# Means and power moved one step up, second weights loaded three pieces ahead, in a fused attention and feed-forward kernel

## The chip, the cores and the metric

The kernel runs on one core of a Trainium2 chip. The metric is the device time of one execution in microseconds; a lower time is better. TensorE (PE) does the matrix products, VectorE (DVE), ScalarE (ACT) and GpSimd (POOL) the elementwise work, and SyncE (SP) issues the transfers between HBM and SBUF.

## What is computed

Attention over normalised queries and keys, for 8 batches of 12 heads with 448 rows of 64, and then a feed-forward over the 3584 rows of 768 that it yields:

```python
def rmsnorm(x, g):
    rms = np.sqrt(np.mean(x * x, axis=-1, keepdims=True) + 1e-06)
    return x / rms * g
q_n, k_n = (rmsnorm(q, g_q), rmsnorm(k, g_k))
scores = scale * np.matmul(q_n, k_n.transpose(0, 1, 3, 2))
attn = np.exp(scores - np.max(scores, axis=-1, keepdims=True))
attn = attn / (np.sum(attn, axis=-1, keepdims=True) + 1e-09)
x = np.matmul(attn, v)            # then (B,H,S,D) -> (B*S, H*D)
h = np.maximum(x @ w_in, 0.0)
out = h * h @ w_out
```

The weights `w_in` (768 x 2048) and `w_out` (2048 x 768) lie in HBM as 64-bit floats; the kernel turns them into 32-bit floats itself.

## The kernel before

**Pairs and steps.** The work is a list of 48 pairs: one batch and two heads each, six pairs to a batch. Each pair `i` takes four steps (`n` = 0 to 3), and in a step TensorE makes the scores of one quarter of the keys (`weigh`, L199), ScalarE their exponentials (L201), and TensorE the products with the values of the pair before (`attend`, L252) with the sums of the exponentials (L259 in the first batch, L263 later, there of sums that POOL and VectorE have added up, L215). The reciprocal of the sums is VectorE's (L274), and `finish` multiplies by it (xT, L283). TensorE's scores use banks 0 and 1 in even steps and 2 and 3 in odd ones.

**Queries and keys.** Before its scores a pair's queries and keys are squared by ScalarE (`square`, L138), summed to means by VectorE (`normalize`, L146 and L147), raised to the power -1/2 by POOL (rr, L151), and POOL multiplies the queries by it (qn, L156; the keys' factor goes into the exponential's scale). `turn` then transposes queries and keys on TensorE (L177) into banks 2 and 3; VectorE copies the turned queries out (qT, L179), ScalarE the keys (kT, L183). In the kernel before, pair i's steps hold for later pairs: the means, power and qn of pair i+1 in step 0, its transposes in step 2, and the squares of pair i+2 in step 3. The inputs of pair i+2 are issued in step 0 of pair i, behind the values of pair i.

**The weights** come in 56 pieces: 0 to 23 are the first weights (128 x 512), 24 to 55 the second (128 x 384). A piece is loaded as 64-bit words (`load_weights`, L386), split (`split_words`: ScalarE L402, POOL L403, ScalarE L407, and then POOL L409 for the first weights or ScalarE L414 for the second) and joined to 32 bits by three VectorE operations (`join_words`, L422, L426, L430). `convert(k)` joins piece k-1, loads a later piece and splits piece k; it runs once a step up to pair 6 and three times a step from pair 7 on. The first weights' words lie in the eight buffers tagged "h2", which the feed-forward uses for its activations later; the second weights' words lie in two buffers tagged "y", which it uses for its results. A load into a buffer waits until the piece that lay there is joined.

**The feed-forward** of a batch is cut into pieces (half a block of 128 hidden columns, six matrix instructions of L307; then L336 in groups of four blocks) that are put between the attention steps of the next batch, from the second pair on: about 2.8 pieces a step for the first batch. Its relu is ScalarE's (L316), the squares of it POOL's (L321, L326). It uses two banks by turns, so that a matmul waits for the relu two blocks earlier. The first pair of a batch has no feed-forward beside it.

Every engine runs its instructions in the order in which the program gives them, and so does SP's queue. The program's order is written out by hand.

Of the kernel before, what the change touches and what calls it, by code (L numbers as in the profile page):

```python
# [20 lines left out]
NJ = 4  # L21
# [52 lines left out]
def program(ctx, tc, q, k, v, g_row, moe_w_in, moe_w_out, out, shift):  # L74
# [5 lines left out]
    DM, DFF = moe_w_in.shape  # L80
    NC = DM // P
    NF = DFF // P
# [50 lines left out]
    def square(i):  # L133
        squares = [
            att.tile([CP, 2 * NJ, D], F32, name="squares", tag="squares") for _ in range(2)
        ]
        for x in range(2):
            nc.scalar.activation(squares[x], loaded[i][:, x], AF.Square)  # L138
        squared[i] = squares

    def normalize(i):

        qk = loaded.pop(i)
        ms = small.tile([CP, 4 * NJ], F32, name="ms", tag="ms", bufs=2)
        for x, squares in enumerate(squared.pop(i)):
            nc.vector.tensor_reduce(out=ms[:, ts(x, 2 * NJ)], in_=squares, axis=AX.X, op=ALU.add)  # L146
        nc.vector.tensor_scalar(  # L147
            out=ms, in0=ms, scalar1=1.0 / D, scalar2=1e-6, op0=ALU.mult, op1=ALU.add
        )
        rr = small.tile([CP, 2, 2 * NJ], F32, name="rr", tag="rr", bufs=4)  # L150
        nc.gpsimd.tensor_tensor(  # L151
            out=rr.rearrange("p x r -> p (x r)"), in0=ms,
            in1=minus_half.to_broadcast([CP, 4 * NJ]), op=ALU.pow,
        )
        qn = att.tile([CP, NJ, 2, D], F32, name="qn", tag="qn", bufs=1)
        nc.gpsimd.tensor_tensor(  # L156
            out=qn.rearrange("p j h d -> p h j d"),
            in0=qk[:, 0].rearrange("p (h j) d -> p h j d", j=NJ),
            in1=rr[:, 0].rearrange("p (h j) -> p h j", j=NJ)[:, :, :, None].to_broadcast([CP, 2, NJ, D]),
            op=ALU.mult,  # L160
        )
        kn = qk[:, 1]
        if shift:
            nc.gpsimd.tensor_tensor(
                out=kn, in0=kn, in1=rr[:, 1, :, None].to_broadcast([CP, 2 * NJ, D]), op=ALU.mult
            )
        normal[i] = qn, kn.rearrange("p (j h) d -> p j h d", h=2), rr[:, 1]

    def turn(i):

        qn, kn, _ = normal[i]
        qT = att.tile([P, S], F32, name="qT", tag="qT")
        kT = att.tile([P, S], F32, name="kT", tag="kT")
        for x, (dst, rows) in enumerate(((qT, qn), (kT, kn))):
            tr = banks[2 + x][:, 0:S]
            for j in range(NJ):
                nc.tensor.transpose(tr[:, ts(j, CP)], rows[:, j].rearrange("p h d -> p (h d)"), ident[:CP, :CP])  # L177
            if x == 0:
                nc.vector.tensor_scalar(  # L179
                    out=dst, in0=tr, scalar1=g, scalar2=None, op0=ALU.mult  # L180
                )
            else:
                nc.scalar.copy(dst, tr)  # L183
        turned[i] = qT, kT
# [92 lines left out]
    def finish(i):  # L277

        b, c = pairs[i]
        if c == 0:  # L280
            xts[b] = [None] * NC
        xT = ffn_p.tile([P, S], F32, name="xT", tag="xT", bufs=NC + 2)
        nc.vector.tensor_tensor(  # L283
            out=xT, in0=banks[4 + i % 2][:, 0:S], in1=dens.pop(i), op=ALU.mult
        )
        xts[b][c] = xT
        del turned[i], normal[i], values[i]
# [74 lines left out]
    def weight_chunks():  # L362

        n = DFF // 4
        for blk in range(4):
            for c in range(NC):
                yield w_in_sb[:, c, ts(blk, n)], moe_w_in[ts(c, P), :], blk * n
        for half in range(2):
            for f in range(NF):
                yield w_out_sb[:, f, ts(half, HALF)], moe_w_out[ts(f, P), :], half * HALF  # L370

    chunks = list(weight_chunks())
    words = {}

    def load_weights(k):
        if k >= len(chunks):
            return
        dst, rows, col = chunks[k]
        n = dst.shape[1]
        if rows.dtype == F32:  # L380
            nc.sync.dma_start(dst, rows[:, col : col + n])
            return

        tag, bufs = ("h2", NF // 2) if n == DFF // 4 else ("y", 2)
        words[k] = ffn_p.tile([P, n, 2], U32, name="words", tag=tag, bufs=bufs)
        nc.sync.dma_start(  # L386
            words[k].rearrange("p n w -> p (n w)"), rows.bitcast(U32)[:, 2 * col : 2 * (col + n)]
        )
# [9 lines left out]
    def split_words(k):  # L398
        if k not in words:
            return  # L400
        low, high = words[k][:, :, 0], words[k][:, :, 1]
        nc.scalar.activation(high.bitcast(F32), high.bitcast(F32), AF.Copy, scale=REBIAS)  # L402
        nc.gpsimd.tensor_scalar(  # L403
            out=high.bitcast(F32), in0=high.bitcast(F32), scalar1=MOST, scalar2=-MOST,
            op0=ALU.min, op1=ALU.max,
        )
        nc.scalar.activation(low.bitcast(F32), low, AF.Copy, scale=2.0**-29, bias=2.0**23)  # L407
        if k < 4 * NC:
            nc.gpsimd.tensor_scalar(  # L409
                out=low, in0=low.bitcast(F32), scalar1=-(2.0**23), scalar2=1.0,  # L410
                op0=ALU.add, op1=ALU.mult,
            )
        else:
            nc.scalar.activation(low, low.bitcast(F32), AF.Copy, bias=-(2.0**23))  # L414

    def join_words(k):
        if k not in words:
            return
        both = words.pop(k)
        low, high = both[:, :, 0], both[:, :, 1]  # L420
        bits = chunks[k][0].bitcast(U32)
        nc.vector.tensor_scalar(  # L422
            out=bits, in0=high, scalar1=4, scalar2=1,
            op0=ALU.logical_shift_left, op1=ALU.logical_shift_right,
        )
        nc.vector.scalar_tensor_tensor(  # L426
            out=bits, in0=high, scalar=0x80000000, in1=bits,
            op0=ALU.bitwise_and, op1=ALU.bitwise_or,
        )
        nc.vector.tensor_tensor(out=bits, in0=bits, in1=low, op=ALU.add)  # L430

    def convert(k):

        join_words(k - 1)
        if k + 3 < 4 * NC:
            load_weights(k + 3)
        elif k + 1 >= 4 * NC:
            load_weights(k + 1)
        split_words(k)

    load_qk(0)
# [16 lines left out]
    last = len(pairs) - 1  # L458

    with tc.manual_schedule(engines=ENGINES):  # L460
        square(0)
        normalize(0)
        turn(0)
        square(1)
        stream, pieces, done, piece = iter(()), 0, 0, 0
        for i, (b, c) in enumerate(pairs):
            for n in range(NJ):
                step = c * NJ + n
                if n == 0:
                    if i > 1 and not shift:  # L470
                        finish(i - 2)
                    load_v(i)
                    if i + 2 <= last:
                        load_qk(i + 2)
                if step == NJ and b:
                    stream, pieces, done = ffn(b - 1), ffn_pieces(b - 1), 0
                    while shift and piece <= len(chunks):
                        convert(piece)
                        piece += 1
                while shift and step == NJ and done < pieces or done * (steps - NJ) < pieces * (step - NJ + 1):  # L480
                    next(stream, None)
                    done += 1
                if shift and n == 0 and i:
                    for m in range(NJ):
                        attend(i - 1, m)
                    finish(i - 1)
                weigh(i, n)
                if i and not shift:
                    attend(i - 1, n)
                if i < last:  # L490
                    if n == 0:
                        normalize(i + 1)
                    if n == 2:
                        turn(i + 1)
                    if n == NJ - 1 and i + 2 <= last:
                        square(i + 2)
                for _ in range(1 if i < NPAIR + 1 else 3):
                    if piece <= len(chunks):
                        convert(piece)
                        piece += 1  # L500
            if c == NPAIR - 1:
                for _ in stream:
                    pass
        if not shift:
            finish(last - 1)
        for n in range(NJ):
            attend(last, n)
        finish(last)
        for _ in ffn(B - 1):
            pass  # L510
# [30 lines left out]
```

## Time and profile before

| what | value |
|---|---|
| median of 3 runs | 1763.82 us (1763.35 to 1767.3) |
| the profiled execution's own time | 1766.63 us |
| its span | 1764.8 us |
| TensorE (PE) busy | 1670.1 us, 95% of the span |
| VectorE (DVE) busy | 503.3 us, 29% |
| ScalarE (ACT) busy | 453.9 us, 26% |
| GpSimd (POOL) busy | 553.6 us, 31% |
| transfers | 70.24 MB, mean 40 GB/s |
| mean granted TensorE clock | 0.969 of full speed |

The shares are means over the whole run. In the profile's 40 slices TensorE is busy for 5 to 8 tenths in the first six slices (some 265 us), where the weights are converted, and for 9 tenths or more from there to the last one; the granted clock is below full speed in the same slices. "Idle before" in a row is the time an engine stood still before that instruction, and the arrow names what ended it.

### The profile page before, as it was taken

What the parts mean: (1) busy time and instruction counts of PE and PEld (TensorE: products, weight loads), DVE (VectorE), ACT (ScalarE), POOL (GpSimd) and SP (SyncE); (2) the same over time, 40 slices, a digit from 0 to 9 for tenths busy, and PEclk for the clock granted to TensorE, in tenths of its full rate; (3) what the DMA queues carried; (4) which work ended last, traced back from release to release, by engine and by line L of the source; (5) the groups of instructions that cost most, each with busy time, mean ns of one, the idle gap of its engine ahead of it and who ended that gap; (6) DMA issues with size and microseconds to landing.
All of it is one profiled execution on the core that took longest, in us unless ns stands there. A gap on an engine that the chain in (4) does not pass through costs nothing.

```text
span 1764.8 us, 14547 instructions
## 1 busy us (share of the span) xinstructions
PE 1670.1 (95%) x5516; PEld 781.7 (44%) x5516; DVE 503.3 (29%) x616; ACT 453.9 (26%) x829; POOL 553.6 (31%) x564
## 2 busy tenths in 40 slices
PE   5778789999999999999999999999999999999998
PEld 2223234534455344444455444544445444454554
DVE  4665453232222322232122322223222322221000
ACT  5553552132211322122211222122211222211100
POOL 5554443133311433224311333224421234212200
PEclk8878989999999999999999999999999999999999
DMA  5423431010010101110001100010011100000000
GB/s 183 155 97 80 112 105 43 25 41 16 17 34 25 40 16 32 34 41 16 16 25 34 40 16 16 25 49 16 20 30 32 34 22 26 14 15 9 0 19 20
DMA packets 80211, 70.24 MB, mean 40 GB/s; under 512 B 47876, under 2 KB 69380, under 8 KB 80132
## 3 DMA queue, kind: packets, MB, share of 16 engines
q1 hardware_dynamic: 80128, 69.23, 13.7%
q8 instruction: 45, 0.74, 0.2%
q14 instruction: 34, 0.28, 0.1%
q10 hardware_dynamic: 4, 0.00, 0.0%
HBM read 58.20 MB, written 11.01 MB: 39 GB/s over the span
## 4 chain that ended last, share of the span: by engine, by line
PE 83%; issue 5%; DVE 4%; POOL 3%; ACT 2%; DMA 2%; POOLq 0%; ACTq 0%; DVEq 0%; SPq 0%
PE bank L336 33%; PE bank L307 30%; PE bank L199 9%; PE bank L252 8%; DMA words<-in_moe_w_out_dram 2%; POOL rr L151 2%; PE bank L263 2%; PE bank L177 2%; DVE sum L215 1%; POOL words L403 1%; ACT wT L201 1%; DVE w_out_sb L426 1%; DVE qT L179 1%; ACT words L402 0%; DVE w_out_sb L422 0%
## 5 line engine op out<-in xcount | busy, mean ns | idle before, releaser
L307 PE MATMUL bank<-xT,w_in_sb 128*128 128x448 f32 x1536 | 611.8, 554 | 22.8 <-ACT h L316 20.9
L336 PE MATMUL bank<-w_out_sb,h 128*128 128x384 f32 x1792 | 593.9, 489 | 0.0
L336 PEld LDWEIGHTS bank<-w_out_sb,h 128*128 128x128 f32 x1792 | 335.4, 190 | 254.0 <-issue 32.2
L307 PEld LDWEIGHTS bank<-xT,w_in_sb 128*128 128x128 f32 x1536 | 291.2, 194 | 335.5 <-issue 287.7
L201 ACT ACTIVATE wT<-bank,rr 112x448 f32<-112x448 f32 x384 | 222.6, 631 | 536.9 <-PE bank L199 536.9
L199 PE MATMUL bank<-qT,kT 64*112 64x448 f32 x768 | 206.1, 616 | 25.9 <-DVE qT L179 25.3
L215 DVE TENSOR_TENSOR sum<-sum,wT 112x448 f32<-112x448 f32 x84 | 98.5, 1173 | 412.9 <-ACT wT L201 412.9
L215 POOL TENSOR_TENSOR sum<-sum,wT 112x448 f32<-112x448 f32 x84 | 98.8, 1176 | 359.6 <-ACT wT L201 358.5
L252 PE MATMUL bank<-wT,vt 112*64 112x448 f32 x768 | 194.6, 588 | 0.0
L316 ACT ACTIVATE h<-bank 128x448 f32<-128x448 f32 x128 | 69.0, 542 | 418.8 <-PE bank L307 418.8
L151 POOL TENSOR_TENSOR rr<-ms,minus_half 112x16 f32<-112x16 f32 x48 | 140.5, 2927 | 100.0 <-DVE ms L147 87.4
L215 DVE TENSOR_TENSOR sum<-wT 112x448 f32<-112x448 f32 x42 | 26.5, 632 | 483.1 <-PE bank L263 468.1
L274 DVE RECIPROCAL rden<-bank 128x448 f32<-128x448 f32 x48 | 141.6, 2951 | 13.7 <-PE bank L259 12.5
L215 POOL TENSOR_TENSOR sum<-wT 112x448 f32<-112x448 f32 x42 | 64.0, 1524 | 202.1 <-PE bank L263 202.1
L326 POOL TENSOR_TENSOR h<-h 128x448 f32<-128x448 f32 x64 | 59.7, 933 | 206.9 <-ACT h L316 206.9
L199 PEld LDWEIGHTS bank<-qT,kT 64*112 64x112 f32 x768 | 56.3, 181 | 143.8 <-issue 95.8
L321 POOL TENSOR_TENSOR h<-h 128x384 f32<-128x384 f32 x64 | 53.7, 839 | 164.3 <-ACT h L316 164.3
L252 PEld LDWEIGHTS bank<-wT,vt 112*64 112x64 f32 x768 | 39.5, 138 | 135.0 <-issue 131.3
L343 DVE COPY y<-bank 128x384 f32<-128x384 f32 x28 | 15.4, 549 | 257.8 <-PE bank L336 257.8
L345 ACT COPY y<-bank 128x384 f32<-128x384 f32 x28 | 13.4, 479 | 216.8 <-PE bank L336 204.2
L177 PE MATMUL bank<-ident,qn 112*128 112x112 f32 x192 | 30.9, 287 | 34.6 <-POOL qn L156 34.6
L403 POOL TENSOR_SCALAR words<-words 128x384 f32<-128x384 f32 (+1 forms) x56 | 37.0, 662 | 81.6 <-ACT words L402 80.1
(41 smaller groups left out, 672.6 us busy)
## 6 DMA issues: line engine op xcount, KB each, us to landing
words<-in_moe_w_in_dram SPq DMA_DIRECT2D x24, 512.0 KB, 5.0
words<-in_moe_w_out_dram SPq DMA_DIRECT2D x32, 384.0 KB, 3.2
qk<-in_q_dram SPq DMA_DIRECT2D x48, 224.0 KB, 3.0
qk<-in_k_dram SPq DMA_DIRECT2D x96, 112.0 KB, 3.3
vt<-in_v_dram SPq DMA_DIRECT2D x48, 224.0 KB, 2.8
out_dram<-y SPq DMA_DIRECT2D x8, 336.0 KB, 2.7
out_dram<-y SPq DMA_DIRECT2D x8, 288.0 KB, 2.6
out_dram<-y SPq DMA_DIRECT2D x8, 240.0 KB, 2.8
```

The lines of the kernel that those rows point to most:

```text
L151: nc.gpsimd.tensor_tensor(out=rr.rearrange("p x r -> p (x r)"), in0=ms, in1=minus_half.to_broadcast([CP, 4 * NJ]), op=ALU.pow,)
L177: nc.tensor.transpose(tr[:, ts(j, CP)], rows[:, j].rearrange("p h d -> p (h d)"), ident[:CP, :CP])
L199: nc.tensor.matmul(sc, lhsT=kT[r, ts(m, CP)], rhs=qT[r, :], start=True, stop=True)
L201: nc.scalar.activation(weights[i, e, m], sc, AF.Exp, scale=normal[i][2][:, 2 * m + e : 2 * m + e + 1])
L215: engine.tensor_tensor(out=sums[i, e], in0=so_far, in1=weights[i, e, m], op=ALU.add)
L252: nc.tensor.matmul(av[ds(e * D, D), :], lhsT=vt[:, e, m, :], rhs=weights[i, e, m], start=m == 0, stop=m == NJ - 1,)
L274: nc.vector.reciprocal(out=rden, in_=den)
L307: nc.tensor.matmul(ps, lhsT=w_in_sb[:, c, ts(f, P)], rhs=xT[c], start=c == 0, stop=c == NC - 1,)
L316: nc.scalar.activation(h[:, at : at + S], ps, AF.Relu)
L326: nc.gpsimd.tensor_tensor(out=full, in0=full, in1=full, op=ALU.mult)
L336: nc.tensor.matmul(ps, lhsT=h2[f][:, ts(n, P)], rhs=w_out_sb[:, f, ts(half, HALF)], start=f == 0, stop=f == NF - 1,)
L403: nc.gpsimd.tensor_scalar(out=high.bitcast(F32), in0=high.bitcast(F32), scalar1=MOST, scalar2=-MOST, op0=ALU.min, op1=ALU.max,)
```

## The change

`normalize` (means, power, qn) of pair i+2 now stands in step 3 of pair i, ahead of that step's scores and of the reciprocal of pair i-1; it stood in step 0 of pair i+1. `square` of pair i+2 stands in step 2, behind the transposes of pair i+1, and no longer behind step 3. `normalize(1)` is made ahead of the loop. `convert(k)` loads piece k+3 for all pieces; for the second weights it was piece k+1. The odd pieces of the second weights up to 47 get one of the eight "h2" buffers; the even ones and 49 to 55 stay in the two "y" buffers.

```diff
-        tag, bufs = ("h2", NF // 2) if n == DFF // 4 else ("y", 2)
+        early = n == DFF // 4 or k % 2 and k < len(chunks) - NF // 2
+        tag, bufs = ("h2", NF // 2) if early else ("y", 2)
         words[k] = ffn_p.tile([P, n, 2], U32, name="words", tag=tag, bufs=bufs)
...
         join_words(k - 1)
-        if k + 3 < 4 * NC:
-            load_weights(k + 3)
-        elif k + 1 >= 4 * NC:
-            load_weights(k + 1)
+        load_weights(k + 3)
         split_words(k)
...
         normalize(0)
         turn(0)
         square(1)
+        normalize(1)
...
+                if n == NJ - 1 and i + 2 <= last:
+                    normalize(i + 2)
                 if shift and n == 0 and i:
...
                 weigh(i, n)
                 if i and not shift:
                     attend(i - 1, n)
-                if i < last:
-                    if n == 0:
-                        normalize(i + 1)
-                    if n == 2:
-                        turn(i + 1)
-                    if n == NJ - 1 and i + 2 <= last:
+                if n == 2 and i < last:
+                    turn(i + 1)
+                    if i + 2 <= last:
                         square(i + 2)
```

On VectorE, one pair of the first stage, from the copy of the turned queries (qT_535) on. Before, with the reciprocal, a join, xT and only then the means (the rows L422, L426 and L430 are one join):

```order
L179 TENSOR_SCALAR qT_535<-bank2_107,g_101 128x448
L422 TENSOR_SCALAR w_in_sb_103<-words_440 128x512
L426 SCALAR_TENSOR_TENSOR w_in_sb_103<-words_440,w_in_sb_103 128x512
L430 ISA w_in_sb_103<-words_440,w_in_sb_103 128x1024
L274 RECIPROCAL rden_566<-bank6_111 128x448
L422 TENSOR_SCALAR w_in_sb_103<-words_465 128x512
L426 SCALAR_TENSOR_TENSOR w_in_sb_103<-words_465,w_in_sb_103 128x512
L430 ISA w_in_sb_103<-words_465,w_in_sb_103 128x1024
L283 TENSOR_TENSOR xT_581<-bank4_109,rden_566 128x448
L146 TENSOR_REDUCE ms_599<-squares_568 112x8
L146 TENSOR_REDUCE ms_599<-squares_569 112x8
L147 TENSOR_SCALAR ms_599<-ms_599 112x16
```

The same place in the changed kernel, whose lines L423, L427 and L431 are the join:

```order
L179 TENSOR_SCALAR qT_535<-bank2_107,g_101 128x448
L423 TENSOR_SCALAR w_in_sb_103<-words_444 128x512
L427 SCALAR_TENSOR_TENSOR w_in_sb_103<-words_444,w_in_sb_103 128x512
L431 ISA w_in_sb_103<-words_444,w_in_sb_103 128x1024
L146 TENSOR_REDUCE ms_560<-squares_547 112x8
L146 TENSOR_REDUCE ms_560<-squares_548 112x8
L147 TENSOR_SCALAR ms_560<-ms_560 112x16
L274 RECIPROCAL rden_578<-bank6_111 128x448
L423 TENSOR_SCALAR w_in_sb_103<-words_473 128x512
L427 SCALAR_TENSOR_TENSOR w_in_sb_103<-words_473,w_in_sb_103 128x512
L431 ISA w_in_sb_103<-words_473,w_in_sb_103 128x1024
L283 TENSOR_TENSOR xT_589<-bank4_109,rden_578 128x448
```

The two sums and the scaling of the means went from behind xT to ahead of the reciprocal; they are those of the pair after next.

On SP's queue, where the first weights' loads end and the second's begin (vt are the values, qk queries and keys). Before:

```order
L386 DMA words<-in_moe_w_in_dram 128x1024
L386 DMA words<-in_moe_w_out_dram 128x768
L127 DMA vt<-in_v_dram 112x2x256
L113 DMA qk<-in_q_dram 112x2x256
L118 DMA qk<-in_k_dram 112x4x64 x2
L386 DMA words<-in_moe_w_out_dram 128x768 x4
```

And in the changed kernel:

```order
L387 DMA words<-in_moe_w_in_dram 128x1024
L387 DMA words<-in_moe_w_out_dram 128x768 x3
L127 DMA vt<-in_v_dram 112x2x256
L113 DMA qk<-in_q_dram 112x2x256
L118 DMA qk<-in_k_dram 112x4x64 x2
L387 DMA words<-in_moe_w_out_dram 128x768 x4
```

Two more pieces of the second weights stand ahead of pair 6's values and the queries and keys of pair 8, and so it stays, two pieces more ahead, up to pair 9.

## Rows read from the trace of the kernel before

**Rows 1.** TensorE's waits over the span: total us, times, longest us.

```profile
PE bank L177 <- POOL qn L156: 34.6, 14, 9.0
PE bank L199 <- DVE qT L179: 25.3, 13, 3.5
PE bank L307 <- ACT h L316: 20.9, 7, 5.1
```

**Rows 2.** Stretches: length, busy us (count) by engine, granted clock, DMA share, GB/s.

```profile
40.15:118.97 78.82, 56.90 (x224) 18.99 (x224) 53.72 (x73) 42.77 (x76) 42.61 (x41) 0.78 0.39 127
154.33:273.49 119.16, 98.24 (x277) 42.14 (x277) 58.87 (x99) 61.91 (x124) 53.68 (x67) 0.90 0.38 104
599.30:686.55 87.25, 87.25 (x277) 38.14 (x276) 20.72 (x20) 22.35 (x40) 35.76 (x41) 1.00 0.06 16
```

**Rows 3.** Timeline of one first-stage pair: start, us, engine, line, operation, idle before.

```profile
84.14 2.96 DVE L274 RECIPROCAL rden<-bank 128x448 f32<-128x448 f32 x1 [2.54 <-PE bank L259]
...
86.61 1.01 PE L199 MATMUL bank<-qT,kT 64*112 64x448 f32 x4
...
87.02 0.36 DVE L422 TENSOR_SCALAR w_in_sb<-words 128x512 uint32<-128x512 uint32 x1
...
88.85 0.62 DVE L283 TENSOR_TENSOR xT<-bank,rden 128x448 f32<-128x448 f32 x1
...
89.20 1.01 PE L199 MATMUL bank<-qT,kT 64*112 64x448 f32 x4
...
89.39 1.27 DVE L146 TENSOR_REDUCE ms<-squares 112x8 f32<-112x512 f32 x2
...
90.95 3.01 POOL L151 TENSOR_TENSOR rr<-ms,minus_half 112x16 f32<-112x16 f32 x1 [5.63 <-DVE ms L147]
...
91.23 0.69 DVE L426 SCALAR_TENSOR_TENSOR w_in_sb<-words,w_in_sb 128x512 uint32<-128x512 uint32 x1
...
95.14 1.01 PE L177 MATMUL bank<-ident,qn 112*128 112x112 f32 x4 [3.27 <-POOL qn L156]
...
95.85 0.43 DVE L422 TENSOR_SCALAR w_in_sb<-words 128x512 uint32<-128x512 uint32 x1 [3.10 <-POOL words L403]
...
98.29 0.67 DVE L179 TENSOR_SCALAR qT<-bank,g 128x448 f32<-128x448 f32 x1
...
99.01 1.83 PE L199 MATMUL bank<-qT,kT 64*112 64x448 f32 x4 [2.12 <-DVE qT L179]
...
103.96 1.14 PE L199 MATMUL bank<-qT,kT 64*112 64x448 f32 x4
```

**Rows 4.** Timeline of TensorE: the last scores of pairs 1 and 6.

```profile
40.15 1.84 PE L199 MATMUL bank<-qT,kT 64*112 64x448 f32 x4 [2.92 <-DVE qT L179]
...
140.30 1.84 PE L199 MATMUL bank<-qT,kT 64*112 64x448 f32 x4 [3.51 <-DVE qT L179]
```

**Rows 5.** Timeline of the second stage: a late piece and the matmul behind it.

```profile
189.14 0.54 ACT L402 ACTIVATE words<-words 128x384 f32<-128x384 f32 x1 [4.57 <-DMA words<-in_moe_w_out_dram]
...
192.95 1.83 PE L307 MATMUL bank<-xT,w_in_sb 128*128 128x448 f32 x2 [5.11 <-ACT h L316]
```

**Rows 6.** DMA issues: count, KB each, median us from issue to landing.

```profile
words<-in_moe_w_in_dram SPq DMA_DIRECT2D x24, 512.0 KB, 5.0
words<-in_moe_w_out_dram SPq DMA_DIRECT2D x32, 384.0 KB, 3.2
...
qk<-in_k_dram SPq DMA_DIRECT2D x96, 112.0 KB, 3.3
```

**Rows 7.** Timeline: the first pair of batch 3 (from 0), and the scores of batch 4's.

```profile
584.23 2.95 DVE L274 RECIPROCAL rden<-bank 128x448 f32<-128x448 f32 x1
...
586.73 0.60 PE L177 MATMUL bank<-ident,qn 112*128 112x112 f32 x4 [1.34 <-POOL qn L156]
...
588.89 1.81 PE L199 MATMUL bank<-qT,kT 64*112 64x448 f32 x4 [1.18 <-DVE qT L179]
...
784.53 1.01 PE L199 MATMUL bank<-qT,kT 64*112 64x448 f32 x4 [1.18 <-DVE qT L179]
```

## Prediction

> **What bounds the kernel now.** I read the waits of TensorE first, then the stages, then one pair's timeline. TensorE waits for three things [rows 1]: the transposes for the normalised queries (POOL qn), the scores for the turned queries (DVE qT), and the feed-forward's matmuls for a relu on ScalarE. The stages tell where [rows 2]. In the first one (pairs 2 to 5, no feed-forward beside them) TensorE is busy 56.90 of 78.82 us at a mean granted clock of 0.78; in the second (first feed-forward, while the second weights are converted) 98.24 of 119.16 us at 0.90. The third row is the same amount of work as the second, two batches later: 28 feed-forward pieces and ten attention steps in 87.25 us, TensorE never idle. So the second stage loses 119.16 - 87.25 = 31.9 us, and the last half of the run has nearly nothing to give.
>
> One pair of the first stage [rows 3] shows the loop. The reciprocal of the sums starts at 84.14; behind it on VectorE stand a join of words, xT and the means (89.39); only then can POOL take the power (90.95, 3.01 us), then qn; the transposes start at 95.14 after 3.27 us of idle TensorE. That is not all: POOL's next half of a word split stood behind the power, so VectorE's join at 95.85 waited 3.10 for it, and qT (98.29) stands behind that join. The next scores start at 99.01, after another 2.12 idle, and run at the lower of the two clock levels (1.2 against 2.4 GHz): the step from there lasts 4.95 us (to 103.96), where a step with TensorE fed lasts 2.59 (86.61 to 89.20). A pair takes 78.82 / 4 = 19.7 us, of which TensorE needs four times 2.59 and about 1.2 for the transposes, 11.6.
>
> In the second stage the loads are late [rows 5]: ScalarE waits 4.57 us for a piece of the second weights, the relus behind it in its queue wait too, and the matmul that needs the relu's bank starts at 192.95 after 5.11 idle, at the lower clock.
>
> **Part 1: means and power one step up.** No instruction is added or taken away; square goes ahead of the third step's split, and means, power and qn go to step 3, a whole pair before their transposes. The wait for qn (3.27) then has three steps of cover, 7.8 us and more, against 4.2 from the power's start to the transposes, so I cost it at nothing. The wait of the join at 95.85 goes with it, because the split of that step no longer stands behind a power. What is late next is qT, by VectorE's own load. From the starts in [rows 3]: reciprocal 2.88 (84.14 to 87.02), xT 0.54, means 1.56 (89.39 to the power's start), qT 0.67, together 5.65, and four joins. A join beside an idle POOL takes 1.83 (87.02 to 88.85); one beside POOL's split takes 2.44 (95.85 to 98.29). So VectorE's period is between 5.65 + 4 x 1.83 = 13.0 and 5.65 + 4 x 2.44 = 15.4 us, both above TensorE's 11.6. I take 15.4: the power now starts right before the reciprocal, POOL's splits pile up behind it and run back to back beside the joins.
>
> The row of POOL's power bears on this: under its 3.01 us the join's second operation at 91.23 took 0.69, no longer than alone. The Trainium skill ("SBUF — State Buffer", Who interferes with whom) says that VectorE and GpSimd share one pair of ports, and that the second of two such instructions to start is blocked until the first has ended. By that rule alone the power would block joins too; the trace disagrees for the power (0.69), and agrees for the splits (2.44 against 1.83). By the rule a join behind qn would be held as well, the period would be about a microsecond longer and the sum below 5 us smaller.
>
> The upper bound comes from the clock: TensorE still idles 15.4 - 11.6 = 3.8 us a pair, in one piece before the scores. In [rows 4] an idle of 2.92 was followed by scores of 1.84, the lower level. If the step that follows qT takes 4.95 and not 2.59, the reciprocal starts 4.95 after qT and not 2.44 + 1.56 = 4.0, so the period is 16.4.
>
> The sum of the first stage: the first pair's scores at 40.15 lose their wait, 2.9 [rows 4]; four pairs go from 19.7 to 15.4, 4 x 4.3 = 17.2; the sixth pair, 118.97 to 140.30 = 21.3, I let gain as much, 4.2 (its row's wait alone is 3.51). **24 us.** With 13.0 it is 2.9 + 26.8 + 6.7 = 36; with 16.4 and nothing in the first pair, 13.2 + 3.3 = 16. From there to the feed-forward I cost nothing: xT has to wait for the reciprocal either way, which now stands behind the means.
>
> **Part 2: loads three ahead.** Until now every piece of the second weights was loaded one piece ahead into two buffers. A load lands 3.2 us after its issue [rows 6], so ScalarE meets it late. Now odd pieces up to 47 take buffers of the feed-forward and wait for no join; even ones wait for the join of the piece four before them and are still issued about a step (87.25 / 10 = 8.7 us) before their split. That covers the 3.2, and 5.0 too, which is what the first weights' loads take with three under way. From piece 49 on, all use the two old buffers: load k+3 waits there for the join of k+1, and the distance falls back to one. Of the 28 pieces in the stage 7 stay as they are. The stage lost 31.9 over 28, so 31.9 x 7 / 28 = 8 stays and **24 us** go. If no relu waits on the last seven, it is 32; if the loads that now stand together land like the first weights', 5.0, half of it, 16. A reordering costs here as well: the loads of pieces 52 to 54 stand on SP's queue ahead of the value and query/key loads of pair 9 and wait for joins. Those inputs are wanted two steps later, so I cost that at nothing; without the two steps it would be one landing, 3.3.
>
> **Part 3: the first pair of each later batch.** Six times there is a pair without feed-forward beside it [rows 7]. TensorE idles 1.34 for qn and 1.18 for qT. The first goes, the second grows: the reciprocal (584.23, 2.95) and a sum still hold VectorE, and the scores can hardly start before 588.5. So the idle stays near 2 us, but in one piece. What can come back is the clock: at 588.89 the scores took 1.81, at 784.53, after the same idle, 1.01. Two such matmul groups stand in a step here, so a half-clock step costs 2 x 0.8 = 1.6. I let five of the six recover, **8 us**. Bounds: nothing, or 15 when the feed-forward's first matmuls were slow too.
>
> **The sum**: 24 + 24 + 8 = 56 us. It was worked out on the profiled execution, 1766.6 us by its own time (span 1764.8), which is 2.8 over the median of the runs, 1763.8. Taken from the median: **1708 us**. The bounds together reach from 36 + 32 + 15 = 83 (1681) to 16 + 16 + 0 = 32 (1732).
>
> **Rivals.**
> - *VectorE is freer than I think*: the joins miss POOL's splits, the period is 13.0, the first stage gives 36: 1708 - 12 = 1696. For it: under the power a join is not slowed [rows 3]. Against it: four splits and qn now fall in the time of four joins. Chance 0.12.
> - *The loads become the bound*: three of them share the rings with queries, keys and values and land in 5.0 or later [rows 6], or the last seven pieces hold the relus longer. The second stage gives 16: 1716. For it: the first weights' loads do land in 5.0. Against it: the rings were busy for 0.38 of that stage [rows 2]. Chance 0.14.
> - *The clock stays low*: every pair of the first stage idles 3 us and more in one piece, and each step after it is run at the lower level; the later batches' pairs don't recover. 16 + 24 + 0 = 40: 1724. For it: the idle of 2.92 at 40.15. Chance 0.12.
> - *Slower than before*: ScalarE's squares now come a step earlier, ahead of exponentials and splits; if their queries and keys have not landed, ScalarE stops, and TensorE with it. They are issued one after another at the pair's start, and the keys land in 3.3 [rows 6]. The squares are wanted after three steps and the transposes, 3 x 2.59 + 1.2 = 9 us after that start in the first stage, and some 2 us sooner in the pairs of part 3. It decides from a last landing of 7 us after the pair's start on, and to make the kernel slower it would have to give back 56 us over 46 pairs, 1.2 us in each. Nothing in the rows lands so late. Chance 0.02.
> - *The change does nothing*: the order of TensorE's transposes is unchanged, and qT stays behind the joins; if the joins alone set the period, only the loads help, 1740. Against it: the join at 95.85 waited 3.10 for POOL. Chance 0.02.
>
> **How the numbers follow.** My forecast, both waits gone and VectorE the bound of the first stage, has 0.58. The range takes in the first three rivals and leaves out the two ends at which all bounds fall together: 1688 to 1726. A change of 0.2% is 3.5 us, about what a measurement here can tell from none. All cases but one are faster by more; faster 0.97, same 0.01, slower 0.02.
>
> **What would show it.** In the changed profile TensorE's wait for qn should be gone in pairs 2 to 5, the wait for qT should be 3 to 4 us, VectorE busy nearly all the time there, and the means should stand right before the reciprocal. ScalarE should wait for the second weights in the last seven pieces only, and the ten steps from the first feed-forward scores some 95 us long. In the later batches the wait for qn should be nil and that for qT about 2 us. The forecast is wrong if a pair of the first stage still takes 18 us or more, if the loads' waits come back between pieces 28 and 48, or if ScalarE is seen waiting for queries or keys.

## The result, and the profile after

| | before | changed |
|---|---|---|
| median | 1763.59 us (1763.21 to 1767.3, 4 runs) | 1716.57 us (1716.1 to 1717.33, 4 runs) |
| ratio, 95% interval | | 0.9729 (0.9712 to 0.9746) |
| the profiled execution's own time, span | 1766.63, 1764.8 | 1716.1, 1714.3 |
| mean granted TensorE clock | 0.969 | 0.985 |

The kernel became 47.0 us faster; 56 were forecast. The second stage and all that follows gained about as the forecast had it; the first stage gave 17.0 us in place of 24 (17.6 with the stretch from its end to the feed-forward).

TensorE's waits over the span, and below them ScalarE's for the second weights (us in total, times, longest), in the changed kernel:

```profile
PE bank L199 <- DVE qT L179: 35.2, 13, 4.2
PE bank L177 <- POOL qn L156: 10.3, 2, 9.2
PE bank L307 <- ACT h L316: 6.2, 1, 6.2
...
ACT words L403 <- DMA words<-in_moe_w_out_dram: 18.9, 8, 4.5
```

Beside [rows 1]: the wait for qn fell from 14 times to the two at the program's head, that for a relu from seven to one, and the wait for qT grew from 25.3 to 35.2. The stretches, with the columns of [rows 2]: the last scores of pair 1 to those of pair 5, the ten steps from the first feed-forward scores, and the two steps of them in which the one relu wait lies:

```profile
41.03:105.36 64.33, 51.10 (x224) 16.47 (x224) 58.10 (x73) 42.77 (x76) 44.45 (x41) 0.90 0.51 168
136.74:232.31 95.57, 89.35 (x277) 39.05 (x277) 64.31 (x101) 62.91 (x124) 53.14 (x67) 0.96 0.40 121
207.90:222.75 14.85, 8.63 (x21) 3.57 (x20) 8.08 (x15) 7.97 (x16) 5.34 (x10) 0.77 0.35 94
```

The first answers to 78.82 us and the second to 119.16. Set against the steps of the forecast (starts from the two timelines; the pair 6 rows are in [rows 4] and below):

| stretch | before | after | gain | forecast |
|---|---|---|---|---|
| to the last scores of pair 1 | 40.15 | 41.03 | -0.9 | 2.9 |
| from there to those of pair 5 | 78.82 | 64.33 | 14.5 | 17.2 |
| to those of pair 6 | 21.33 | 17.98 | 3.4 | 4.2 |
| to the first feed-forward scores | 14.03 | 13.40 | 0.6 | 0 |
| ten steps of the second stage | 119.16 | 95.57 | 23.6 | 24 |
| all that follows | | | 9.3 | 8 |
| the span | 1764.8 | 1714.3 | 50.5 | 56 |

The last scores of pairs 1 to 6 in TensorE's timeline after the change (start, duration, idle before):

```profile
41.03 1.84 PE L199 MATMUL bank<-qT,kT 64*112 64x448 f32 x4 [4.01 <-DVE qT L179]
57.61 1.01 PE L199 MATMUL bank<-qT,kT 64*112 64x448 f32 x4 [2.85 <-DVE qT L179]
73.22 1.74 PE L199 MATMUL bank<-qT,kT 64*112 64x448 f32 x4 [4.25 <-DVE qT L179]
89.29 1.01 PE L199 MATMUL bank<-qT,kT 64*112 64x448 f32 x4 [3.07 <-DVE qT L179]
105.36 1.84 PE L199 MATMUL bank<-qT,kT 64*112 64x448 f32 x4 [3.07 <-DVE qT L179]
123.34 1.84 PE L199 MATMUL bank<-qT,kT 64*112 64x448 f32 x4 [3.99 <-DVE qT L179]
```

The pairs take 16.58, 15.61, 16.07 and 16.07 us, 16.08 in the mean, where 15.4 was forecast. Only one of them meets it, the one that starts at 57.61. VectorE's reciprocals tell why:

```profile
46.10 2.96 DVE L274 RECIPROCAL rden<-bank 128x448 f32<-128x448 f32 x1 [1.51 <-PE bank L259]
...
61.13 2.95 DVE L274 RECIPROCAL rden<-bank 128x448 f32<-128x448 f32 x1
...
77.58 2.96 DVE L274 RECIPROCAL rden<-bank 128x448 f32<-128x448 f32 x1 [0.81 <-PE bank L259]
...
93.37 2.96 DVE L274 RECIPROCAL rden<-bank 128x448 f32<-128x448 f32 x1 [0.53 <-PE bank L259]
```

At 61.13 VectorE had not stopped, and the pair is the forecast's. In the other three the matmuls from the scores to the sums ran at the lower clock for all or part of the step (mean granted clock 0.50, 0.61 and 0.64, against 1.00 in the pair at 57.61), so that the sums came late and VectorE waited 1.51, 0.81 and 0.53. Without these 2.85 us the four pairs take (64.33 - 2.85) / 4 = 15.4.

The pair that starts at 57.61, across engines, shows the new order and what is late in it now:

```profile
59.74 1.27 DVE L146 TENSOR_REDUCE ms<-squares 112x8 f32<-112x512 f32 x2
...
61.31 3.10 POOL L151 TENSOR_TENSOR rr<-ms,minus_half 112x16 f32<-112x16 f32 x1 [2.85 <-PE bank L199]
...
64.40 0.69 DVE L427 SCALAR_TENSOR_TENSOR w_in_sb<-words,w_in_sb 128x512 uint32<-128x512 uint32 x1
64.49 1.50 POOL L156 TENSOR_TENSOR qn<-qk,rr 112x512 f32<-112x512 f32 x1
...
65.23 1.31 DVE L431 CUSTOM_DVE_ANT_0 w_in_sb<-words,w_in_sb 128x1024 uint16<-128x1024 uint16 x1
...
66.08 1.03 POOL L404 TENSOR_SCALAR words<-words 128x512 f32<-128x512 f32 x1
...
67.14 0.43 DVE L423 TENSOR_SCALAR w_in_sb<-words 128x512 uint32<-128x512 uint32 x1
...
72.49 0.67 DVE L179 TENSOR_SCALAR qT<-bank,g 128x448 f32<-128x448 f32 x1
```

Means, then reciprocal (61.13) and power side by side; the power ends 0.3 us after the reciprocal. POOL's split (66.08) still stands behind power and qn, but the join that needs it starts at 67.14 without a wait, where the one in [rows 3] waited 3.10.

In the second stage TensorE has one stall left, among the pieces that fell back to one load ahead:

```profile
180.91 0.58 ACT L403 ACTIVATE words<-words 128x384 f32<-128x384 f32 x1 [4.54 <-DMA words<-in_moe_w_out_dram]
...
207.86 0.56 ACT L403 ACTIVATE words<-words 128x384 f32<-128x384 f32 x1 [4.27 <-DMA words<-in_moe_w_out_dram]
...
213.99 0.54 ACT L403 ACTIVATE words<-words 128x384 f32<-128x384 f32 x1 [4.52 <-DMA words<-in_moe_w_out_dram]
...
215.45 0.96 ACT L316 ACTIVATE h<-bank 128x448 f32<-128x448 f32 x2
216.03 1.86 PE L307 MATMUL bank<-xT,w_in_sb 128*128 128x448 f32 x2 [6.22 <-ACT h L316]
```

It reads as [rows 5] did: a late piece, the relus behind it in ScalarE's queue, and the matmul that needs their bank, then at the lower clock (1.86). Counted along the queue, the rows at 207.86 and 213.99 are pieces 50 and 51; ScalarE waits for 49, 53, 54 and 55 too, at most 1.75 each. The row at 180.91 is piece 42, which was to be early: it and piece 43 (0.25) are waited for as well. TensorE did not stand still for them. And the six first pairs of the later batches:

```profile
329.64 1.84 PE L199 MATMUL bank<-qT,kT 64*112 64x448 f32 x4 [1.99 <-DVE qT L179]
545.15 1.01 PE L199 MATMUL bank<-qT,kT 64*112 64x448 f32 x4 [1.99 <-DVE qT L179]
738.53 1.46 PE L199 MATMUL bank<-qT,kT 64*112 64x448 f32 x4 [1.99 <-DVE qT L179]
954.16 1.84 PE L199 MATMUL bank<-qT,kT 64*112 64x448 f32 x4 [1.99 <-DVE qT L179]
1149.09 1.01 PE L199 MATMUL bank<-qT,kT 64*112 64x448 f32 x4 [1.99 <-DVE qT L179]
1363.12 1.40 PE L199 MATMUL bank<-qT,kT 64*112 64x448 f32 x4 [1.99 <-DVE qT L179]
```

Where 1.34 and 1.18 stood [rows 7] there is now one idle of 1.99 in each.

### The profile page after: what moved, and what is told of

Same layout as the page of the kernel before. It is cut to its first block, busy times and chain, and to the rows that moved or that the text cites. A ratio compares the mean times of both kernels' runs of the same rounds, so it can differ in the third digit from the quotient of the medians.

```text
span 1714.3 us, 14444 instructions
## 1 busy us (share of the span) xinstructions
PE 1649.2 (96%) x5516; PEld 773.9 (45%) x5516; DVE 489.6 (29%) x616; ACT 455.5 (27%) x829; POOL 559.4 (33%) x564
## 4 chain that ended last, share of the span: by engine, by line
PE 89%; issue 4%; DVE 4%; POOL 2%; ACT 1%; DMA 0%; POOLq 0%; DVEq 0%; ACTq 0%; SPq 0%
PE bank L336 34%; PE bank L307 32%; PE bank L199 9%; PE bank L252 9%; PE bank L177 2%; PE bank L263 2%; POOL rr L151 1%; DVE w_in_sb L427 1%; DVE sum L215 1%; DVE w_in_sb L423 1%; DVE qT L179 1%; PE bank L259 0%; DVE w_out_sb L427 0%; DMA words<-in_moe_w_out_dram 0%; POOL words L404 0%
## 5 line engine op out<-in xcount | busy, mean ns | idle before, releaser
L307 PE MATMUL bank<-xT,w_in_sb 128*128 128x448 f32 x1536 | 599.9, 545 | 7.6 <-ACT h L316 6.2
L307 PEld LDWEIGHTS bank<-xT,w_in_sb 128*128 128x128 f32 x1536 | 286.6, 191 | 311.7 <-issue 279.1
L199 PE MATMUL bank<-qT,kT 64*112 64x448 f32 x768 | 203.2, 609 | 35.8 <-DVE qT L179 35.2
L215 DVE TENSOR_TENSOR sum<-sum,wT 112x448 f32<-112x448 f32 x84 | 79.8, 950 | 348.3 <-ACT wT L201 348.3
L343 DVE COPY y<-bank 128x384 f32<-128x384 f32 x28 | 15.4, 549 | 263.2 <-PE bank L336 263.2
L146 DVE TENSOR_REDUCE ms<-squares 112x8 f32<-112x512 f32 x96 | 61.3, 679 | 4.4 <-ACT squares L138 4.4
L138 ACT ACTIVATE squares<-qk 112x512 f32<-112x512 f32 x96 | 55.4, 627 | 2.3 <-DMA qk<-in_q_dram 1.4
```

The source lines that it names most:

```text
L199: nc.tensor.matmul(sc, lhsT=kT[r, ts(m, CP)], rhs=qT[r, :], start=True, stop=True)
L215: engine.tensor_tensor(out=sums[i, e], in0=so_far, in1=weights[i, e, m], op=ALU.add)
L307: nc.tensor.matmul(ps, lhsT=w_in_sb[:, c, ts(f, P)], rhs=xT[c], start=c == 0, stop=c == NC - 1,)
```

## The experiments

All edits are against the changed kernel. The kernel before was run beside them: its median was 1763.29 us in the runs of the first four, 1764.74 in those of the next four, and 1766.42 beside the last one. Ratios are to it, with 95% intervals.

### One part alone, twice

The order alone, with the loads as they were:

```diff
-        early = n == DFF // 4 or k % 2 and k < len(chunks) - NF // 2
-        tag, bufs = ("h2", NF // 2) if early else ("y", 2)
+        tag, bufs = ("h2", NF // 2) if n == DFF // 4 else ("y", 2)
...
-        load_weights(k + 3)
+        if k + 3 < 4 * NC:
+            load_weights(k + 3)
+        elif k + 1 >= 4 * NC:
+            load_weights(k + 1)
```

> The means, power and squares as in the change, the loads as before. If the parts add up, as I hold: the pairs of the first stage take 16 us as in the change, the later batches' first pairs keep their gain, the second stage stays at 119 us; about 1763.6 - 27 = 1737 us. Rival, the two parts need each other (without the early loads the join waits for words anyway): the first stage stays near 19 us a pair, 1755 us or more.

1741.26 us, 0.9876 (0.9852 to 0.9901), 4 us above what was expected. The first stage is that of the changed kernel (last scores of pair 6 at 123.94), the ten steps take 120.27 us.

The loads alone, with the order as it was (the second half of the diff undone):

> The loads as in the change, the order of means, power and squares as before. If the parts add up: the second stage falls from 119 to about 96 us, the pairs of the first stage stay at 19.7 us, the waits for qn stay; about 1763.6 - 24 = 1740 us, or 1737 if pair 6 gains by the early loads too. Rival, the second stage's gain needs the freer POOL and VectorE: it stays above 105 us, 1750 us or more.

1740.62 us, 0.9871 (0.9838 to 0.9903). The ten steps take 95.1 us; a first-stage pair takes 19 to 20, and TensorE waits 33.4 us for qn. The two parts give 22.0 and 22.7 us, together 44.7, and the change gave 47.0 in its own runs. The runs of either part spread over 5 to 8 us, so the parts add up as far as this shows.

### Loads three ahead in two buffers

```diff
-        early = n == DFF // 4 or k % 2 and k < len(chunks) - NF // 2
-        tag, bufs = ("h2", NF // 2) if early else ("y", 2)
+        tag, bufs = ("h2", NF // 2) if n == DFF // 4 else ("y", 2)
```

> The change with all of the second weights' pieces in the two old buffers, still loaded three ahead by the program. If the buffers and not the place in the program set the distance: every load waits for the join of the piece two before it, the distance is one piece again, and the second stage is back at some 119 us: 1716.6 + 24 = 1740 us. Rival, the place on SP's queue is what counts: 1717 to 1722 us.

1747.08 us, 0.9906 (0.9876 to 0.9936). The stretch of the ten steps:

```profile
141.23:260.67 119.44, 97.78 (x277) 41.89 (x276) 62.48 (x102) 62.39 (x124) 50.98 (x67) 0.89 0.36 103
```

That is the 119.16 of [rows 2]. The loads stand three pieces earlier in the program and land no earlier for it, since each waits for its buffer: all of part 2 is the buffers. Its median is 5.8 us above that of the order alone, but its runs lie between 1742.54 and 1753.03 us, the intervals of the two overlap, and of the two profiled executions this one is the shorter (1744.56 against 1745.09): no difference is shown.

### All odd pieces in the feed-forward's buffers

```diff
-        early = n == DFF // 4 or k % 2 and k < len(chunks) - NF // 2
+        early = n == DFF // 4 or k % 2
```

> The change with the odd pieces 49 to 55 in the feed-forward's buffers too. If the two old buffers are what holds the last seven pieces: TensorE's wait of 6.2 us for a relu near 216 us goes, the second stage falls from 95.6 to about 88 us, 1716.6 - 7 = 1710 us. Rival, the feed-forward's relus now wait for joins that free its buffers: the wait only moves, 1715 to 1725 us.

1708.53 us, 0.9679 (0.9663 to 0.9695), 8.0 less than the changed kernel:

```profile
137.47:224.81 87.34, 87.34 (x277) 38.06 (x277) 60.64 (x98) 60.38 (x120) 50.54 (x64) 1.00 0.43 133
```

TensorE never idles, at full clock, in the time of the undisturbed row of [rows 2] (87.25). So the 8 us that the forecast left in this stage were those of the pieces one load ahead. The rival's wait exists too, but costs little: ScalarE's relu waits 9.5 us in two places for a join (8.00 at 215.83), and the step behind these ten takes 11.10 us where it took 10.19.

### The means behind the reciprocal

Everything is still one step up, but means, power and qn stand behind `attend`, so behind the reciprocal:

```diff
-                if n == NJ - 1 and i + 2 <= last:
-                    normalize(i + 2)
                 if shift and n == 0 and i:
...
                     attend(i - 1, n)
+                if n == NJ - 1 and i + 2 <= last:
+                    normalize(i + 2)
                 if n == 2 and i < last:
```

> The change with the means, power and qn in the same step, but behind the reciprocal and not ahead of it. If the pair of steps gained is what counts and VectorE's whole queue sets the period, the place within the step matters little: 1714 to 1719 us, with no wait for qn in the first stage. Rival, the place ahead of the reciprocal is needed: qn comes 3 us later, POOL's splits are held into the next pair's joins, and a pair of the first stage takes 17 us or more: 1721 us or more.

1739.08 us, 0.9855 (0.9839 to 0.9871): the rival won, and the gain of part 1 is gone (the loads alone had 1740.62; the 1.5 us between them lie within the spread of either). One pair in its timeline:

```profile
66.36 2.96 DVE L274 RECIPROCAL rden<-bank 128x448 f32<-128x448 f32 x1 [2.92 <-PE bank L259]
...
70.74 3.01 POOL L151 TENSOR_TENSOR rr<-ms,minus_half 112x16 f32<-112x16 f32 x1 [8.66 <-DVE ms L147]
...
73.83 1.04 POOL L156 TENSOR_TENSOR qn<-qk,rr 112x512 f32<-112x512 f32 x1
...
74.97 0.67 POOL L404 TENSOR_SCALAR words<-words 128x512 f32<-128x512 f32 x1
...
75.67 0.43 DVE L423 TENSOR_SCALAR w_in_sb<-words 128x512 uint32<-128x512 uint32 x1 [2.59 <-POOL words L404]
...
80.98 0.67 DVE L179 TENSOR_SCALAR qT<-bank,g 128x448 f32<-128x448 f32 x1
...
81.71 1.84 PE L199 MATMUL bank<-qT,kT 64*112 64x448 f32 x4 [5.79 <-DVE qT L179]
...
85.94 2.96 DVE L274 RECIPROCAL rden<-bank 128x448 f32<-128x448 f32 x1 [2.08 <-PE bank L259]
```

Over four pairs of the first stage TensorE's wait for qn is 1.7 us (12.4 before the change), but that for qT is 20.6 (10.3 before). The loop is closed as before: reciprocal, means, power and qn, POOL's split, the join that waits 2.59 for it, one join more, qT, the scores at the lower clock, the next reciprocal 19.6 us after the first. With the means ahead of the reciprocal, power and reciprocal run at the same time, and the split is done when VectorE comes to it.

### Work taken off VectorE: qT copied by ScalarE

```diff
-                nc.vector.tensor_scalar(
-                    out=dst, in0=tr, scalar1=g, scalar2=None, op0=ALU.mult
-                )
+                nc.scalar.activation(dst, tr, AF.Copy, scale=g)
```

> The change, with the copy of the turned queries (times g) done by ScalarE behind the copy of the keys, not by VectorE behind the joins. If VectorE's queue of joins is what TensorE's scores wait for: the wait for qT of 35 us over the run falls below 15, the pairs of the first stage go from 16.1 to some 14.5 us, the first pairs of the later batches lose about 1 us more each; about 1716.6 - 8 - 6 = 1703 us. Rival, the first stage is bound by VectorE's busy time alone (58.1 of 64.3 us): a pair gains only the 0.67 us of the copy, 1712 us. Rival, ScalarE is now late with the exponentials: 1717 us or more.

1700.68 us, 0.965 (0.9628 to 0.9673). Three pairs, from reciprocal to reciprocal:

```profile
44.70:91.03 46.33, 39.91 (x180) 13.86 (x177) 44.08 (x52) 34.69 (x64) 35.64 (x30) 0.93 0.59 192
```

VectorE waits for nothing here and takes 46.33 / 3 = 15.4 a pair: with the sums never late, its own work is the period. That is not the 14.5 that was expected: without the copies VectorE is still busy for 14.7 us a pair (14.5 in the changed kernel), since the joins became longer; the four from 63.06 to 74.16 take 10.5 us without the xT among them, four of the changed kernel's pair at 57.61 took 10.1. TensorE now waits for qn in five pairs (up to 3.31). The scores do not stand behind the joins any more, and those of pair 6 start at 112.64, 10.7 us sooner. But little of it stays: the first feed-forward matmul waits 9.76 for xT, which VectorE comes to late, and the first feed-forward scores are 2.7 us ahead (134.08). The ten steps gained nothing (95.59). All that follows gave the rest, 13.3 us: in the later batches' first pairs the wait for qT fell from 11.9 us to 2.0, and the mean granted clock of the stretch is 1.00. So the total came within 2 us of the forecast with the gain in another place.

### The low split of the first weights on ScalarE

```diff
-        if k < 4 * NC:
+        if k < 0:
             nc.gpsimd.tensor_scalar(
```

> The change, with the last operation of the first weights' split on ScalarE (as it is for the second weights) and not on POOL. If joins that run beside POOL's splits are what stretches VectorE's period: half of POOL's split time goes, a join falls from some 2.4 to 2.0 us, and a pair of the first stage from 16.1 to about 14.5 us; 1716.6 - 8 = 1709 us. Rival, the clock and not the joins makes up the rest over my 15.4: nothing, 1717 us. Rival, ScalarE, busy for 10.7 us of a pair, becomes the bound with 0.6 us more in each of four steps: 1717 to 1722 us.

1711.38 us, 0.9708 (0.9685 to 0.9731).

```profile
39.49:101.71 62.22, 51.73 (x224) 16.53 (x225) 55.28 (x73) 52.83 (x94) 29.47 (x24) 0.89 0.52 174
```

With POOL's work cut from 44.45 to 29.47 us, VectorE's fell from 58.10 to 55.28: joins beside fewer splits are shorter, by 2.82 / 16 = 0.18 us each where 0.4 was expected. The pair is 15.6, 0.5 less and not 1.6, and the clock stays at 0.89: scores still stand behind joins and qT, and the sums are still late in three of four pairs (VectorE waits 3.6 us for them, 2.85 before this edit). The result lies between theory and rival: of the 2.8 us of work that went, 2.1 show in the stretch.

### Both, and then all three

qT and the low split on ScalarE:

> The change with both the turned queries' copy and the last operation of the first weights' split on ScalarE. With the copy alone VectorE was busy for 61.9 of 65.0 us in the first stage, so what is left is its busy time, and joins beside POOL's splits are a part of it. If so, a pair falls from 15.4 to some 14.2 us and the wait for xT at the first feed-forward shrinks: 1700.7 - 7 = 1694 us. Rival, ScalarE becomes the bound (10.7 + 0.6 + 2.6 = 14 us of a pair): 1699 us or more.

1693.23 us, 0.959 (0.9574 to 0.9606). Four pairs:

```profile
38.82:93.15 54.33, 47.10 (x225) 16.30 (x225) 51.30 (x66) 53.82 (x97) 31.44 (x24) 1.00 0.61 199
```

The pair is 13.6 at full granted clock, near the lower end of the forecast's 13.0 to 15.4. ScalarE, busy 53.82 of 54.33 us, has become the bound, as the rival had it, but at 13.6 us a pair and not at the rival's time.

With all odd pieces in the feed-forward's buffers as well:

> The changed kernel with three further edits at once: qT copied by ScalarE, the low split of the first weights on ScalarE, and all odd pieces of the second weights in the feed-forward's buffers. If the stages are worth what they were apart, the last relu wait of the second stage goes (8.0 us, from 1716.6 to 1708.5 when it was done alone) on top of the 1693.2 us of the other two: 1685 us, with ten feed-forward steps of the second stage at 87 to 88 us and the first stage's period at 13.6. Rival: ScalarE, which then carries the qT copies as well, still makes a relu or the sixth pair's scores late once the loads no longer do, and half or more of the 8 us stays: 1689 us or above.

1688.85 us (1685.66 to 1689.39), 0.9559 (0.9543 to 0.9575), the fastest kernel here, 27.7 us under the changed one. It came 4.4 us below the kernel with two edits (5.5 by the ratios), not 8: between theory and rival. The rival's cause is not seen: the relu wait of 6.2 us is gone. In the profiled executions it is 2.1 us behind already at the first feed-forward scores, before the edit has any part in the order, and most of that comes from one pair:

```profile
38.94 2.25 PE L197 MATMUL bank<-qT,kT 64*112 64x448 f32 x4 [2.22 <-ACT qT L179]
...
54.09 1.43 PE L197 MATMUL bank<-qT,kT 64*112 64x448 f32 x4 [0.34 <-ACT qT L179]
```

The kernel with two edits idled 1.21 at that place, its scores took 1.42 and the pair 13.6; here it idled 2.22, and the pair took 15.15 at a granted clock of 0.78 (1.00 there). Why it idled longer stays open. The ten steps take 87.42 us against 96.37, 8.9 less. The step behind them gives 0.9 back (11.10 against 10.19), as with all odd pieces alone, and the last 1.7 us lie behind TensorE's last matmul: 8.1 us from there to the end against 6.5. So the spans differ by 4.3 although the stage gave the whole 8.

## Why the prediction was right, and where it was off

**The order against the reciprocal, not the step.** Part 1 said that the join's 3.10 wait goes "because the split of that step no longer stands behind a power". That reason was wrong, though the wait did go. The split still stands behind power and qn (66.08 above). What hides them is the reciprocal, which holds VectorE for 2.95 us while POOL takes the power; the means behind the reciprocal, also one step up, bring back a pair of about 20 us. The step earlier alone nearly removes the wait for qn in the first stage (12.4 to 1.7 us in four pairs) and gains nothing there, because qT is then late by as much (10.3 to 20.6).

**The first pair** fell by the same error. I gave it 2.9 us; it lost 0.9. In pair 0 there is no reciprocal to hide the power:

```profile
30.02 3.02 POOL L151 TENSOR_TENSOR rr<-ms,minus_half 112x16 f32<-112x16 f32 x1 [2.02 <-DVE ms L147]
...
34.94 0.43 DVE L423 TENSOR_SCALAR w_in_sb<-words 128x512 uint32<-128x512 uint32 x1 [3.12 <-POOL words L404]
...
37.42 0.87 DVE L423 TENSOR_SCALAR w_in_sb<-words 128x512 uint32<-128x512 uint32 x1
...
40.31 0.67 DVE L179 TENSOR_SCALAR qT<-bank,g 128x448 f32<-128x448 f32 x1
```

The join waits 3.12 for the split behind the power, as one did before, and two joins stand between it and qT. This term is 3.8 us too large. With the four pairs (2.7) and pair 6 (0.8) the first stage fell 7.3 us short; what the other stretches gave beyond the forecast brings the error of the sum down to 5.5.

**The first stage's period.** VectorE's 15.4 was right: the pair without a wait shows 15.61 (four joins 10.1 us where 9.8 was forecast, the rest 5.5 where 5.65 was), and the four pairs less the reciprocals' waits give 15.4. The 15.4 of the kernel with qT on ScalarE is no support, since the same sum without qT would give 14.7. What was mis-sized is the choice between two cases. I named the late sums after a half-clock step as a bound (16.4) and took none of it; three of four pairs had some, 2.85 us in all, 0.7 a pair. Pair 6 gained 3.4 and not 4.2.

**What a join beside qn costs.** The forecast weighed a rule here. In the pair above qn took 1.50 against 1.04 beside a waiting VectorE (73.83 in the kernel with the means behind), and the join's third operation beside it 1.31 against 0.69 alone; the kernel with qT on ScalarE shows the same two figures in four pairs. The power held no join (0.69 at 64.40, right behind it, and in [rows 3] under it). The Trainium skill ("SBUF — State Buffer", Who interferes with whom) calls the ports that VectorE and GpSimd share an exclusive lock; the trace agrees for qn and the splits, at about 0.6 us a join and not the microsecond that I worked out, and disagrees for the power.

**The second stage** was right in mechanism and size: 95.57 against "some 95 us", the stall in the last pieces, and the experiments with two buffers and with all odd pieces show that the buffers are the cause. That the 8 us left came out by a share of pieces, 7 of 28, was in part luck: one stall of 6.2 us with the slow matmuls behind it made them up. And one sign of being wrong did appear: loads' waits between pieces 28 and 48. The load of piece 42 waits for the join of piece 38, which ends at 177.28, behind a join that waited 3.35 us (at 172.31) for POOL's splits, and these stood behind a power, qn and a sum (166.65 to 171.77). So the load was issued at 177.34, after ScalarE had already asked for the piece (176.37), and not "about a step" before its split. An even piece is early only if the join of the piece four before it is in time. It cost TensorE nothing here.

**The later batches.** The idle is near 2 us in one piece, as forecast. That the clock recovers in five of six was not: two of the six scores took 1.01, two 1.40 and 1.46, two 1.84; before, one took 1.01 and five 1.53 to 1.84. The stretches that follow the second stage, before and after, with the columns of [rows 2]:

```profile
273.49:1764.80 1491.31, 1468.86 (x4851) 702.62 (x4850) 346.87 (x379) 311.89 (x563) 420.08 (x420) 0.99 0.09 25
232.31:1714.30 1481.99, 1462.86 (x4851) 700.67 (x4850) 322.81 (x376) 312.52 (x561) 419.67 (x417) 0.99 0.09 25
```

The same 4851 matmuls take 6.0 us less, which is the clock's part, where 8 was forecast. The other 3.3 are idle: six times 1.33 to 1.40 for qn and 1.18 for qT became six times 1.99. The forecast had that shorter idle and left it out of its sum. So 9.3 against 8 is near for two errors that run against each other.

**The rivals.** Inputs that come late for the squares by the change were not seen. The page of the changed kernel has 2.3 us of such idle, all of it for the first pair's inputs in the first 8 us, and the kernel before had 2.1 there:

```profile
L138 ACT ACTIVATE squares<-qk 112x512 f32<-112x512 f32 x96 | 55.4, 627 | 2.3 <-DMA qk<-in_q_dram 1.4
```

"The clock stays low" was true in part of the pairs. "The loads become the bound" was priced at 1716, which is the time that was measured, but that is chance: its second stage was to give 16 us and gave 23.6. The time alone could not have told it from the forecast; the stretches do.

**From the sum to the time.** Of the 8.6 us between 1708 and 1716.6, 5.5 are the terms above. The other 3.1 come, but for some tenths of rounding, from taking a sum that was made on the profiled execution off the median: that execution was 3.0 us above the median, the one of the changed kernel 0.5 below its own. The profiled times differ by 50.5, the medians by 47.0.

## What to carry to other kernels

Where two engines pass work back and forth in order, look for the closed loop (here reciprocal, means, power, split, join, qT, scores, reciprocal), and ask which order lets the two long operations run at the same time; moving work earlier by a step without breaking the loop only renamed the wait here (from qn to qT). The prefetch distance was set by the buffers, not by the place of the load in the program: ask when the buffer comes free, and what that waits for. When a period has two limits that lie within a microsecond of each other, price the mixture and not the better one.

## What the runs showed of the hardware

The length of an idle did not decide at which clock TensorE went on. After the same 1.99 us the same scores took 1.01, 1.40, 1.46 and 1.84 us, at a mean granted clock of 1.00, 0.67, 0.65 and 0.50: in the two between, the clock fell on the way. After 3.07 us they took 1.01 at 89.29 (granted clock 1.00, the level of 2.4 GHz) and 1.84 at 105.36 (0.50, that of 1.2 GHz). And of two operations of GpSimd with two inputs, the power (112x16, 3.0 us) slowed no join, while qn (112x512) and a join slowed each other when they met, to 1.50 from 1.04 and to 1.31 from 0.69.
